# One layout for the loop's buffer ring, kept open to the end of the kernel

## The chip, the cores and the metric

The kernel runs on one core of a Trainium2 chip. The metric is the device time of one execution in microseconds. Before the change three runs took 781.46, 783.53 and 784.13 us; the median is 783.53.

## The reference, cut to what matters

Three stages follow one another, all in float32.

```python
# 1. attention, per batch and head: a local window of +-16 keys and 24 block summaries
k_sum, v_sum = k.reshape(B,H,nb,32,D).max(3), v.reshape(B,H,nb,32,D).mean(3)
a = softmax([q k^T / 8 inside the window, q k_sum^T / 8 + log 32])
attn = a @ [v, v_sum]                  # B, H, S, D = 4, 8, 768, 64
# 2. feed-forward: 3072 tokens, 512 -> 2048 -> 512
h = x @ w_in;  x = (h * cos(h)) @ w_out
# 3. soft mixture of 8 experts with 4 slots each
logits = x @ phi                       # 3072 x 32
d, c = softmax over tokens, softmax over slots
slot_out[e] = relu((d^T x)[e] @ w1[e]) @ w2[e]     # 512 -> 1024 -> 512
return c @ slot_out
```

## The kernel before

The feed-forward part is the backbone. It runs over 6 blocks of 512 tokens (NB) times 16 tiles of 128 hidden units (NF): 96 slots, and two more to drain. In slot s TensorE (PE) does mm1(s), 12 matmuls of 128x512 (L384, L385, L388), and mm2(s-2), 12 more (L425, L426, L429). Every operand is split in a high and a low float32r half, so a product takes three matmuls. Between them, DVE reduces the angle (L402, L403), ACT takes the sine (L404), DVE multiplies (L409, the tile `a`), ACT casts the high half (L412) and GpSimd (POOL) subtracts for the low half (L413). The weights of a later slot are split in the same way by `split_w`: ACT casts (L372), POOL, or in the first block DVE, subtracts (L373).

Around the backbone the attention of 24 groups (g) is spread, as background steps placed at given slots by `at` and `at2`: scores (sc), maximum (mx), exponentials, normalisation, transposes (tr, L336) that ACT copies (aT, L342), and the value product (av, L354), whose output is the x operand of mm1. Sums over 32 keys or values need loads of their own: kr (keys, reduced by DVE in L170 to ks) and vb (values, reduced by PE in L184 to vs, moved or added by DVE in L193 and L195). From the second batch on, all kr and vb loads go one after the other through one buffer, the tag `v2`: a load waits until the one before has been used. In the first block the 16 weight tiles (w0 to w15) also arrive packed as 64-bit numbers (raw, 1 MB each) and are converted in three steps, ACT (w and cv, L129, L130), DVE (a shift, L136) and POOL (an addition, L141).

After the loop comes the tail: expert weights are loaded in 64 transfers of 512 KB (`grab`, L532), each into a buffer that the loop has used up, and PE does the combine transposes (ct), the first expert product (hp, L809), the second (yp, L842) and the combine (op, L866), whose results leave in 12 transfers (L871).

The order of the work comes from two sources. Up to slot 17 (MAN0) a planner simulates a timeline and orders the instructions of all engines. From slot 17 on, PE and the queue of DMA issues (SP) take the written order, and the planner orders the other engines only. Inside an engine instructions run strictly in order: one that waits holds up everything behind it. A tile of a pool may be written again when all instructions that read it are done; two instructions that use different tiles don't wait for one another.

The parts that the change touches: the pool `ring` (2 buffers by default) with the tags `wih`, `wil`, `woh`, `wol` (hi and lo tiles of 2 KB a partition, 2 buffers each), `gh`, `gl` (3 buffers each) and `a`; the copies aT of the first four groups, which borrow tiles of that ring; the calls of `grab` at the end of the loop; and the pool `tail`, opened in the place of the closed ring, with 7 tiles r0 to r6 for expert weights and the tile cT0 for the first half of the combine operand.

Of the kernel before, what the change touches and what calls it, by code (L numbers as in the profile page):

```python
# [10 lines left out]
F32 = mybir.dt.float32  # L11
F32R = mybir.dt.float32r
# [18 lines left out]
TB = 512  # L31
# [17 lines left out]
NEXP = 12  # L49
WARM1 = 4  # L50
WARM2 = 4
NRING = 7
HB = (-4, 14)
HF = (-6, 10)
OA = 4
# [23 lines left out]
def body(ctx: ExitStack, tc: tile.TileContext, q0, qk, kT, vn, vx, w, phi, ex, cst, out):  # L79
# [7 lines left out]
    ps_acc = ctx.enter_context(tc.tile_pool(name="ps_acc", bufs=1, space=PSUM))  # L87
    ps_h = ctx.enter_context(tc.tile_pool(name="ps_h", bufs=2, space=PSUM))
    ps_m = ctx.enter_context(tc.tile_pool(name="ps_m", bufs=2, space=PSUM))
    ring_cm = tc.tile_pool(name="ring", bufs=2, side="right", reuse_waits="tile")  # L90
    ring = ring_cm.__enter__()
    att_cm = tc.tile_pool(name="att", bufs=2, reuse_waits="tile")
    att = att_cm.__enter__()

# [237 lines left out]
    def att_C(g, j):  # L332
        d = grp[g]
        ps = bank(f"tr{g}_{j}") if g < 4 else ps_m.tile([128, 512], F32, name=f"tr{g}_{j}", tag="m")
        for u in range(4):
            nc.tensor.transpose(ps[:KC, 128 * u:128 * u + 128], d["S"][:, 4 * j + u, :], ident)  # L336
        if g < 4:
            pool, tag, n = ring, ("gh", "gh", "gh", "gl", "gl", "gl", "a", "a")[2 * g + j], 2 if g == 3 else 3
        else:
            pool, tag, n = att, "aT", 2  # L340
        aT = pool.tile([KC, 512], F32, name=f"aT{g}_{j}", tag=tag, bufs=n)
        nc.scalar.copy(aT, ps[:KC, :])  # L342
        d["aT", j] = aT

# [22 lines left out]

    def split_w(f, part, eng=None):
        d, nm = ((wi, "wi"), (wo, "wo"))[part]
        hi = ring.tile([128, 512], F32R, name=f"{nm}h{f}", tag=nm + "h")  # L370
        lo = ring.tile([128, 512], F32R, name=f"{nm}l{f}", tag=nm + "l")
        nc.scalar.copy(hi, W[f][:, part, :])  # L372
        (eng or nc.gpsimd).tensor_tensor(out=lo, in0=W[f][:, part, :], in1=hi, op=ALU.subtract)  # L373
        d[f] = (hi, lo)
# [32 lines left out]
    def act2(s):  # L407
        h, a = hps.pop(s), gs[s]
        nc.vector.tensor_tensor(out=a, in0=h, in1=a, op=ALU.mult)  # L409
        gh = ring.tile([128, TB], F32R, name=f"gh{s}", tag="gh", bufs=3)  # L410
        gl = ring.tile([128, TB], F32R, name=f"gl{s}", tag="gl", bufs=3)
        nc.scalar.copy(gh, a)  # L412
        nc.gpsimd.tensor_tensor(out=gl, in0=a, in1=gh, op=ALU.subtract)  # L413
        gs[s] = (gh, gl)
# [265 lines left out]
    for s in range(NSLOT + LAG):  # L680
        if MAN is not None and s == MAN0:
            guard = tc.manual_schedule(engines=MAN)
            guard.__enter__()
        if s < NSLOT:
            mm1(s)
        if s + 1 < NSLOT:
            split_w((s + 1) % NF, 0, nc.vector if s + 1 < NF else None)
        if 0 <= s - LAG + 1 < NSLOT:
            split_w((s - LAG + 1) % NF, 1)
        if s < NSLOT:  # L690
            act1(s)
        fire(s, 0)
        if s < NSLOT:
            act2(s)
        if s >= LAG:
            mm2(s - LAG)
            if (s - LAG) % NF == NF - 1:
                last = [x2_out(t) for t in range(4)][3]
        fire(s, 1)
        fire(s, 2)  # L700
        if s - LAG >= NSLOT - NF:
            grab(wres, f"w{s - LAG - (NSLOT - NF)}")
    assert not bg, bg
    if guard:
        guard.__exit__(None, None, None)
    grab(xres, "xh", 2, bufs=2)
    grab(xres, "xl", 2, bufs=2)


    ring_cm.__exit__(None, None, None)  # L710
    tail = ctx.enter_context(tc.tile_pool(name="tail", bufs=1, side="right", reuse_waits="tile"))
    for i in range(NRING):
        grab(tail, f"r{i}")

    def cT_mm(j):

# [7 lines left out]
    def cT_split(j):  # L724

        ps = cps.pop(j)
        o = cT[j // 2][:, 512 * (j % 2):512 * (j % 2) + 512]
        nc.scalar.copy(o, ps)
        for r in (slice(32, 64), slice(96, 128)):
            nc.vector.tensor_tensor(out=o[r, :], in0=ps[r, :], in1=o[r, :], op=ALU.subtract)  # L730

    cps = {}
    cT = [tail.tile([128, 1024], F32R, name="cT0", tag="cT0")]


    with tc.issue_after(last.ins):
# [67 lines left out]
    for g in range(2):  # L804
        hp = [ps_acc.tile([128, 512], F32, name=f"hp{g}_{i}", tag=f"acc{2 * g + i}") for i in range(2)]
        for k in range(4):
            for i in range(2):
                for j in range(4):
                    nc.tensor.matmul(hp[i][32 * j:32 * j + 32, :], slT[:, k, :],  # L809
                                     eu[16 * g + 4 * k + j][0][:, 512 * i:512 * i + 512],  # L810
                                     start=k == 0, stop=k == 3)
            for j in range(4):
                release(16 * g + 4 * k + j, 2)
            if g == k == 0:
                cT.extend(place(f"cT{i}", F32R) for i in range(1, NB // 2))
                for j in range(2, NB):
                    cT_split(j)
        hr, t_ = place(f"hr{g}"), place(f"hT{g}").rearrange("p (k c) -> p k c", c=128)
# [14 lines left out]
    for h in range(2):  # L833
# [23 lines left out]
        for i in range(NB):  # L857
            pool, tag, kw = places[(NB * h + i) % 4]
            o = pool.tile([128, 4, 256], F32, name=f"o{h}_{i}", tag=tag, **kw)
            for t in range(2):  # L860
# [1 line left out]
                turn_o += 1  # L862
                ps = pool.tile([128, 512], F32, name=f"op{h}_{i}_{t}", tag=tag)
                for n in range(2):
                    k = 512 * (i % 2) + 256 * t + 128 * n
                    product = nc.tensor.matmul(ps[:, 256 * n:256 * n + 256], cT[i // 2][:, k:k + 128], so[:, c],  # L866
                                               start=True, stop=True)
                if i == 1:
                    before = slot_out, product
# [74 lines left out]
```

## Time and profile before

| | us |
|---|---|
| runs (3) | 781.46, 783.53, 784.13 |
| the profiled execution | 780.9 |
| its span, first to last instruction | 778.9 |
| PE busy | 740.2 |
| DVE busy | 473.6 |
| ACT busy | 433.4 |
| POOL busy | 428.6 |

The granted clock over the span is 0.987 of full speed. The profiled execution lies 2.6 us below the median of the runs. A time in the profile counts from the start of the span. Busy is the time in which an engine ran an instruction; matmuls are pipelined, so neighbouring ones overlap in the timeline, and their pitch is the distance of two starts. In the timeline, the bracket behind an instruction is the idle time of its engine just before it and what ended it.

### The profile page before, as it was taken

The numbers are of one execution on the slowest core, as the hardware profiler recorded it, in microseconds if no ns is written. First come the engines' busy times: TensorE is split into PE (matmuls) and PEld (weight loads), VectorE is DVE, ScalarE is ACT, GpSimd is POOL, SyncE is SP. The second block draws the span as 40 slices with busy tenths as digits, with TensorE's granted clock in tenths as the row PEclk, the third lists the DMA queues.
The fourth block names the chain that finished last, engine by engine and source line by source line (L and its number), as shares of the span: only waits on it lengthen the run. The fifth ranks groups of instructions, "written<-read, shape, count | busy, mean of one in ns | idle before, by whom it ended". The sixth has DMA issues, their size and how long they took to land.

```text
span 778.9 us, 13853 instructions
## 1 busy us (share of the span) xinstructions
PE 740.2 (95%) x5517; PEld 573.5 (74%) x5517; DVE 473.6 (61%) x686; ACT 433.4 (56%) x786; POOL 428.6 (55%) x302
## 2 busy tenths in 40 slices
PE   9977799998999999998999999999999999999994
PEld 7866678776877787776787777778768888786453
DVE  4578896767477576576575684774773444433523
ACT  4979868636465455574465555464554455443222
POOL 2555884365557657556566566665576665752000
PEclk9997999999999999999999999999999999999998
DMA  9988753121120331311211211301101922328978
GB/s 331 396 264 331 271 164 113 42 97 59 48 95 1 100 105 29 121 68 41 87 44 33 72 40 33 111 0 35 33 1 56 392 93 82 109 81 299 371 306 268
DMA packets 35585, 101.69 MB, mean 131 GB/s; under 512 B 3393, under 2 KB 13889, under 8 KB 33473
## 3 DMA queue, kind: packets, MB, share of 16 engines
q1 hardware_dynamic: 35520, 100.81, 36.8%
q8 instruction: 43, 0.70, 0.4%
q14 instruction: 22, 0.17, 0.1%
HBM read 92.54 MB, written 6.29 MB: 127 GB/s over the span
## 4 chain that ended last, share of the span: by engine, by line
PE 63%; DVE 13%; ACT 12%; DMA 6%; issue 4%; SPq 0%; ACTq 0%; DVEq 0%
PE acc L425 8%; PE h L384 8%; PE acc L426 8%; PE h L385 8%; PE acc L429 7%; PE h L388 7%; PE av L354 3%; DVE S L329 2%; DMA qk<-in_qk_dram 2%; PE yp L842 2%; DMA kr<-in_kT_dram 2%; PE sc L286 2%; PE hp L809 2%; ACT a L404 2%; DVE a L403 2%
## 5 line engine op out<-in xcount | busy, mean ns | idle before, releaser
L373 POOL TENSOR_TENSOR wol<-w,woh 128x512 fp32r<-128x512 f32 x96 | 143.9, 1500 | 115.0 <-ACT woh L372 115.0
L413 POOL TENSOR_TENSOR gl<-a,gh 128x512 fp32r<-128x512 f32 x96 | 129.0, 1343 | 83.8 <-ACT gh L412 78.3
L384 PE MATMUL h<-xh,wih 128*128 128x512 f32 x384 | 156.4, 407 | 6.7 <-DVE a L409 6.6
L425 PE MATMUL acc<-woh,gh 128*128 128x512 f32 x384 | 157.4, 410 | 3.5 <-DVE x L448 3.5
L385 PE MATMUL h<-xl,wih 128*128 128x512 f32 x384 | 152.2, 396 | 0.0
L426 PE MATMUL acc<-wol,gh 128*128 128x512 f32 x384 | 152.1, 397 | 0.0
L373 POOL TENSOR_TENSOR wil<-w,wih 128x512 fp32r<-128x512 f32 x81 | 113.9, 1406 | 42.8 <-PE h L388 24.2
L402 DVE TENSOR_SCALAR a<-h 128x512 f32<-128x512 f32 x96 | 65.9, 686 | 115.8 <-PE h L388 110.7
L404 ACT ACTIVATE a<-a,halfpi 128x512 f32<-128x512 f32 x96 | 69.4, 724 | 115.7 <-DVE a L403 115.4
L388 PE MATMUL h<-xh,wil 128*128 128x512 f32 x384 | 104.9, 395 | 0.0
L429 PE MATMUL acc<-woh,gl 128*128 128x512 f32 x384 | 104.6, 393 | 0.0
L409 DVE TENSOR_TENSOR a<-h,a 128x512 f32<-128x512 f32 x96 | 66.1, 689 | 57.0 <-ACT a L404 56.9
L425 PEld LDWEIGHTS acc<-woh,gh 128*128 128x128 f32 x384 | 72.4, 188 | 28.6 <-issue 11.8
L384 PEld LDWEIGHTS h<-xh,wih 128*128 128x128 f32 x384 | 72.7, 189 | 24.6 <-DVE a L409 8.4
L372 ACT CAST wih<-w 128x512 fp32r<-128x512 f32 x96 | 59.2, 617 | 47.2 <-PE h L385 46.4
L388 PEld LDWEIGHTS h<-xh,wil 128*128 128x128 f32 x384 | 72.5, 189 | 16.3 <-issue 0.2
L429 PEld LDWEIGHTS acc<-woh,gl 128*128 128x128 f32 x384 | 72.1, 189 | 16.4 <-issue 0.6
L385 PEld LDWEIGHTS h<-xl,wih 128*128 128x128 f32 x384 | 72.8, 190 | 15.2 <-issue 0.3
L426 PEld LDWEIGHTS acc<-wol,gh 128*128 128x128 f32 x384 | 72.6, 189 | 14.6 <-issue 0.6
L412 ACT CAST gh<-a 128x512 fp32r<-128x512 f32 x96 | 59.3, 619 | 32.8 <-DVE a L409 32.8
L372 ACT CAST woh<-w 128x512 fp32r<-128x512 f32 x96 | 59.1, 616 | 21.7 <-PE acc L429 20.8
L403 DVE SCALAR_TENSOR_TENSOR a<-a,h 128x512 f32<-128x512 f32 x96 | 65.5, 683 | 2.1
(137 smaller groups left out, 945.8 us busy)
## 6 DMA issues: line engine op xcount, KB each, us to landing
ex<-in_ex_dram SPq DMA_DIRECT2D x64, 512.0 KB
raw<-in_w_dram SPq DMA_DIRECT2D x16, 1024.0 KB
qk<-in_qk_dram SPq DMA_DIRECT2D x20, 736.0 KB
v<-in_vx_dram SPq DMA_DIRECT2D x24, 512.0 KB
kr<-in_kT_dram SPq DMA_DIRECT2D x16, 384.0 KB
vb<-in_vn_dram SPq DMA_DIRECT2D x12, 512.0 KB
out_dram<-o SPq DMA_DIRECT2D x12, 512.0 KB
v<-vs SPq DMA_DIRECT2D x40, 48.0 KB
```

The costliest lines, as they stand in the source:

```text
L372: nc.scalar.copy(hi, W[f][:, part, :])
L373: (eng or nc.gpsimd).tensor_tensor(out=lo, in0=W[f][:, part, :], in1=hi, op=ALU.subtract)
L384: nc.tensor.matmul(h, hi[:, c], xh[s // NF][:, t, :], start=t == 0, stop=False)
L385: nc.tensor.matmul(h, hi[:, c], xl[s // NF][:, t, :], start=False, stop=False)
L388: nc.tensor.matmul(h, lo[:, c], xh[s // NF][:, t, :], start=False, stop=t == 3)
L403: nc.vector.scalar_tensor_tensor(out=a, in0=a, scalar=MAGIC, in1=h, op0=ALU.subtract, op1=ALU.subtract)
L404: nc.scalar.activation(a, a, AF.Sin, bias=halfpi, scale=-TWO_PI)
L409: nc.vector.tensor_tensor(out=a, in0=h, in1=a, op=ALU.mult)
L413: nc.gpsimd.tensor_tensor(out=gl, in0=a, in1=gh, op=ALU.subtract)
L425: nc.tensor.matmul(acc[t], gh[:, c], hi, start=f == 0, stop=False)
L426: nc.tensor.matmul(acc[t], gh[:, c], lo, start=False, stop=False)
L429: nc.tensor.matmul(acc[t], gl[:, c], hi, start=False, stop=f == NF - 1)
```

## The change

The ring pool is not closed any more. Its hi and lo tiles become one tile of 4 KB a partition: `wi`, `wo` (2 buffers each) and `g` (3 buffers) in place of six tags. The two copies aT of each of the groups 0 to 2 share one tile `g`. The memory in use is the same. The pool `tail` is gone. In its place the last slots of the loop take the ring's tiles for expert weights: `wi` at slots 94 and 95, `xh` and `xl` at slot 95, `wo` at slots 96 and 97, `g` after the loop; the tiles w0 to w15 are taken one slot earlier in the code. The first two combine tiles cT live in the two `a` tiles.

```diff
--- before.py
+++ after.py
@@ -49,7 +49,6 @@
 NEXP = 12
 WARM1 = 4
 WARM2 = 4
-NRING = 7
 HB = (-4, 14)
 HF = (-6, 10)
 OA = 4
@@ -87,8 +86,7 @@
     ps_acc = ctx.enter_context(tc.tile_pool(name="ps_acc", bufs=1, space=PSUM))
     ps_h = ctx.enter_context(tc.tile_pool(name="ps_h", bufs=2, space=PSUM))
     ps_m = ctx.enter_context(tc.tile_pool(name="ps_m", bufs=2, space=PSUM))
-    ring_cm = tc.tile_pool(name="ring", bufs=2, side="right", reuse_waits="tile")
-    ring = ring_cm.__enter__()
+    ring = ctx.enter_context(tc.tile_pool(name="ring", bufs=2, side="right", reuse_waits="tile"))
     att_cm = tc.tile_pool(name="att", bufs=2, reuse_waits="tile")
     att = att_cm.__enter__()
 
@@ -335,10 +333,14 @@
         for u in range(4):
             nc.tensor.transpose(ps[:KC, 128 * u:128 * u + 128], d["S"][:, 4 * j + u, :], ident)
         if g < 4:
-            pool, tag, n = ring, ("gh", "gh", "gh", "gl", "gl", "gl", "a", "a")[2 * g + j], 2 if g == 3 else 3
+            if g == 3:
+                aT = ring.tile([KC, 512], F32, name=f"aT{g}_{j}", tag="a")
+            else:
+                if j == 0:
+                    d["aTs"] = ring.tile([KC, 2, 512], F32, name=f"aT{g}", tag="g", bufs=3)
+                aT = d["aTs"][:, j, :]
         else:
-            pool, tag, n = att, "aT", 2
-        aT = pool.tile([KC, 512], F32, name=f"aT{g}_{j}", tag=tag, bufs=n)
+            aT = att.tile([KC, 512], F32, name=f"aT{g}_{j}", tag="aT")
         nc.scalar.copy(aT, ps[:KC, :])
         d["aT", j] = aT
 
@@ -367,8 +369,8 @@
 
     def split_w(f, part, eng=None):
         d, nm = ((wi, "wi"), (wo, "wo"))[part]
-        hi = ring.tile([128, 512], F32R, name=f"{nm}h{f}", tag=nm + "h")
-        lo = ring.tile([128, 512], F32R, name=f"{nm}l{f}", tag=nm + "l")
+        hl = ring.tile([128, 2, 512], F32R, name=f"{nm}{f}", tag=nm)
+        hi, lo = hl[:, 0, :], hl[:, 1, :]
         nc.scalar.copy(hi, W[f][:, part, :])
         (eng or nc.gpsimd).tensor_tensor(out=lo, in0=W[f][:, part, :], in1=hi, op=ALU.subtract)
         d[f] = (hi, lo)
@@ -407,8 +409,8 @@
     def act2(s):
         h, a = hps.pop(s), gs[s]
         nc.vector.tensor_tensor(out=a, in0=h, in1=a, op=ALU.mult)
-        gh = ring.tile([128, TB], F32R, name=f"gh{s}", tag="gh", bufs=3)
-        gl = ring.tile([128, TB], F32R, name=f"gl{s}", tag="gl", bufs=3)
+        ghl = ring.tile([128, 2, TB], F32R, name=f"g{s}", tag="g", bufs=3)
+        gh, gl = ghl[:, 0, :], ghl[:, 1, :]
         nc.scalar.copy(gh, a)
         nc.gpsimd.tensor_tensor(out=gl, in0=a, in1=gh, op=ALU.subtract)
         gs[s] = (gh, gl)
@@ -698,19 +700,22 @@
                 last = [x2_out(t) for t in range(4)][3]
         fire(s, 1)
         fire(s, 2)
-        if s - LAG >= NSLOT - NF:
-            grab(wres, f"w{s - LAG - (NSLOT - NF)}")
+
+        f = s - LAG + 1 - (NSLOT - NF)
+        if 0 <= f < NF:
+            grab(wres, f"w{f}")
+        if NSLOT - 2 <= s < NSLOT:
+            grab(ring, "wi", bufs=2)
+        if s == NSLOT - 1:
+            grab(xres, "xh", 2, bufs=2)
+            grab(xres, "xl", 2, bufs=2)
+        if s >= NSLOT:
+            grab(ring, "wo", bufs=2)
     assert not bg, bg
     if guard:
         guard.__exit__(None, None, None)
-    grab(xres, "xh", 2, bufs=2)
-    grab(xres, "xl", 2, bufs=2)
-
-
-    ring_cm.__exit__(None, None, None)
-    tail = ctx.enter_context(tc.tile_pool(name="tail", bufs=1, side="right", reuse_waits="tile"))
-    for i in range(NRING):
-        grab(tail, f"r{i}")
+    for i in range(3):
+        grab(ring, "g", bufs=3)
 
     def cT_mm(j):
 
@@ -724,13 +729,15 @@
     def cT_split(j):
 
         ps = cps.pop(j)
-        o = cT[j // 2][:, 512 * (j % 2):512 * (j % 2) + 512]
+        if j < 2:
+            cT[j] = ring.tile([128, 512], F32R, name=f"cT{j}", tag="a")
+        o = cT[j]
         nc.scalar.copy(o, ps)
         for r in (slice(32, 64), slice(96, 128)):
             nc.vector.tensor_tensor(out=o[r, :], in0=ps[r, :], in1=o[r, :], op=ALU.subtract)
 
     cps = {}
-    cT = [tail.tile([128, 1024], F32R, name="cT0", tag="cT0")]
+    cT = {}
 
 
     with tc.issue_after(last.ins):
@@ -812,7 +819,9 @@
             for j in range(4):
                 release(16 * g + 4 * k + j, 2)
             if g == k == 0:
-                cT.extend(place(f"cT{i}", F32R) for i in range(1, NB // 2))
+                for i in range(2, NB, 2):
+                    t = place(f"cT{i}", F32R)
+                    cT[i], cT[i + 1] = t[:, 0:512], t[:, 512:1024]
                 for j in range(2, NB):
                     cT_split(j)
         hr, t_ = place(f"hr{g}"), place(f"hT{g}").rearrange("p (k c) -> p k c", c=128)
@@ -862,8 +871,8 @@
                 turn_o += 1
                 ps = pool.tile([128, 512], F32, name=f"op{h}_{i}_{t}", tag=tag)
                 for n in range(2):
-                    k = 512 * (i % 2) + 256 * t + 128 * n
-                    product = nc.tensor.matmul(ps[:, 256 * n:256 * n + 256], cT[i // 2][:, k:k + 128], so[:, c],
+                    k = 256 * t + 128 * n
+                    product = nc.tensor.matmul(ps[:, 256 * n:256 * n + 256], cT[i][:, k:k + 128], so[:, c],
                                                start=True, stop=True)
                 if i == 1:
                     before = slot_out, product
```

In the changed kernel the lines between about L104 and L333 are numbered 2 lower and those of the loop 2 higher (L384 is L386, L532 is L534); the tile names lose their h and l, so a cast and a subtraction both write wi5, wo2 or g2.

The change moves instructions where the planner orders them. First ACT, in slot 2. aT4_0 is the copy of group 4's first transpose, w9 and cv9 belong to the conversion of weight tile 9, a2 is the sine of slot 2. Before:

```order
L404 ACTIVATE a2_853<-a2_853,halfpi_90 128x512
L372 CAST wih5_1013<-w5_817 128x512
L342 COPY aT4_0_866<-tr4_0_861 120x512
L129 ACTIVATE w9_1103<-raw9_958 128x1024
L130 ACTIVATE cv9_1104<-raw9_958 128x1024
L412 CAST gh2_888<-a2_853 128x512
L372 CAST woh2_934<-w2_583 128x512
```

After:

```order
L406 ACTIVATE a2_842<-a2_842,halfpi_90 128x512
L127 ACTIVATE w9_1083<-raw9_944 128x1024
L128 ACTIVATE cv9_1084<-raw9_944 128x1024
L344 COPY aT4_0_855<-tr4_0_850 120x512
L414 CAST g2_877<-a2_842 128x512
L374 CAST wo2_921<-w2_580 128x512
L374 CAST wi5_998<-w5_809 128x512
```

The copy now stands behind the conversion of w9, and the cast of weight 5's first half (wih5, now wi5) has moved from in front of both to behind the cast of wo2.

Next DVE, in slots 3 and 4. vs1 is the value sum of the second batch, w11 and w12 are shifts of the conversion, a4 the angle of slot 4. Before:

```order
L136 TENSOR_SCALAR w11_1251<-w11_1251 128x1024
L195 TENSOR_TENSOR vs1_877<-vs1_877,vs1_1_942 128x128
L402 TENSOR_SCALAR a4_1021<-h4_1000 128x512
L403 SCALAR_TENSOR_TENSOR a4_1021<-a4_1021,h4_1000 128x512
L373 TENSOR_TENSOR wil6_1092<-w6_879,wih6_1091 128x512
L136 TENSOR_SCALAR w12_1309<-w12_1309 128x1024
L409 TENSOR_TENSOR a4_1021<-h4_1000,a4_1021 128x512
L363 TENSOR_TENSOR xl1_995<-av4_977,xh1_994 128x2x256
```

After:

```order
L411 TENSOR_TENSOR a3_924<-h3_905,a3_924 128x512
L134 TENSOR_SCALAR w11_1225<-w11_1225 128x1024
L404 TENSOR_SCALAR a4_1004<-h4_985 128x512
L405 SCALAR_TENSOR_TENSOR a4_1004<-a4_1004,h4_985 128x512
L375 TENSOR_TENSOR wi6_1073<-w6_868,wi6_1073 128x512
L411 TENSOR_TENSOR a4_1004<-h4_985,a4_1004 128x512
L134 TENSOR_SCALAR w12_1280<-w12_1280 128x1024
L193 TENSOR_TENSOR vs1_866<-vs1_866,vs1_1_928 128x128
L134 TENSOR_SCALAR w13_1355<-w13_1355 128x1024
```

The addition to vs1 stood right behind the shift of w11; now four operations of slot 4, among them the subtraction for wi6, and the shift of w12 stand in front of it. On PE the matmuls vs1_1 that it waits for moved with it, from inside mm1(4) to the start of mm1(5).

DVE again, in slots 7 and 8. mx6 is the row maximum of group 6, ks11 the last key reduction of the third batch. Before:

```order
L409 TENSOR_TENSOR a7_1224<-h7_1203,a7_1224 128x512
L290 SCALAR_TENSOR_TENSOR S6_1230<-sc6_1_1232,mask2_571 128x480
L298 TENSOR_REDUCE mx6_1276<-S6_1230 128x8
L402 TENSOR_SCALAR a8_1301<-h8_1280 128x512
L170 TENSOR_REDUCE ks11_1732<-kr11_1613 128x24
```

After:

```order
L411 TENSOR_TENSOR a7_1198<-h7_1179,a7_1198 128x512
L288 SCALAR_TENSOR_TENSOR S6_1204<-sc6_1_1206,mask2_568 128x480
L168 TENSOR_REDUCE ks11_1685<-kr11_1571 128x24
L296 TENSOR_REDUCE mx6_1249<-S6_1204 128x8
L404 TENSOR_SCALAR a8_1272<-h8_1253 128x512
```

ks11 has moved in front of mx6 and of slot 8's first step.

## Rows read from the trace of the kernel before

**Rows 1.** The page, part 1: engine, busy us, share of the span, instructions

```profile
PE 740.2 (95%) x5517; PEld 573.5 (74%) x5517; DVE 473.6 (61%) x686; ACT 433.4 (56%) x786; POOL 428.6 (55%) x302
```

**Rows 2.** Stretches: length, busy us (PE PEld DVE ACT POOL), clock, DMA share

```profile
80.00:100.00 20.00, 15.70 (x118) 11.94 (x117) 17.63 (x17) 16.51 (x24) 19.11 (x10) 0.91 0.76 271
...
180.00:200.00 20.00, 17.04 (x122) 13.20 (x120) 15.24 (x22) 12.53 (x21) 12.64 (x10) 1.00 0.08 27
200.00:700.00 500.00, 490.91 (x3201) 388.20 (x3200) 303.74 (x436) 270.05 (x442) 310.73 (x225) 1.00 0.22 74
720.00:750.00 30.00, 29.53 (x383) 14.47 (x386) 13.62 (x31) 5.78 (x13) 0.00 (x0) 1.00 1.00 386
```

**Rows 3.** Waits of PE and ACT, 200 to 705: us in total, times, longest

```profile
PE h L384 <- DVE a L409: 3.4, 3, 1.1
...
ACT wih L372 <- PE h L385: 43.1, 45, 1.8
```

**Rows 4.** Timeline of PE: start, us, line, operation, idle time before and releaser

```profile
78.09 0.65 PE L336 MATMUL tr<-ident,S 128*120 128x128 f32 x4
...
85.04 1.15 PE L354 MATMUL av<-aT,v 120*64 120x64 f32 x32 [1.36 <-ACT aT L342]
89.13 0.77 PE L336 MATMUL tr<-ident,S 128*120 128x128 f32 x4 [2.94 <-DVE vs L195]
...
90.55 0.63 PE L425 MATMUL acc<-woh,gh 128*128 128x512 f32 x1
90.98 0.63 PE L426 MATMUL acc<-wol,gh 128*128 128x512 f32 x1
...
98.48 0.65 PE L184 MATMUL vs<-vb,avg 128*32 128x128 f32 x16
...
100.26 0.40 PE L384 MATMUL h<-xh,wih 128*128 128x512 f32 x1
100.49 0.40 PE L385 MATMUL h<-xl,wih 128*128 128x512 f32 x1
...
139.90 0.50 PE L384 MATMUL h<-xh,wih 128*128 128x512 f32 x1
```

**Rows 5.** The line that issues the expert loads: ns min/median/max, first and last

```profile
L532 SPq DMA_DIRECT2D ex<-in_ex_dram x64: 327/328/1144, 587.5 to 744.0; - x64
```

**Rows 6.** Timeline of ACT, slot 2

```profile
77.46 0.58 ACT L342 COPY aT<-tr 120x512 f32<-120x512 f32 x1
77.94 1.15 ACT L129 ACTIVATE w<-raw 128x1024 f32<-128x1024 f32 x1
78.99 1.14 ACT L130 ACTIVATE cv<-raw 128x1024 int32<-128x1024 uint32 x1
```

**Rows 7.** Timeline of DVE, slots 2 to 10

```profile
79.11 0.69 DVE L136 TENSOR_SCALAR w<-w 128x1024 int32<-128x1024 int32 x1 [1.15 <-ACT w L129]
...
88.80 0.27 DVE L195 TENSOR_TENSOR vs<-vs,vs 128x128 f32<-128x128 f32 x1
...
90.32 1.52 DVE L373 TENSOR_TENSOR wil<-w,wih 128x512 fp32r<-128x512 f32 x1
91.76 2.87 DVE L136 TENSOR_SCALAR w<-w 128x1024 int32<-128x1024 int32 x1
...
116.84 1.15 DVE L298 TENSOR_REDUCE mx<-S 128x8 f32<-128x960 f32 x1
...
120.28 0.95 DVE L170 TENSOR_REDUCE ks<-kr 128x24 f32<-128x768 f32 x1 [1.05 <-DMA kr<-in_kT_dram]
...
124.80 0.69 DVE L409 TENSOR_TENSOR a<-h,a 128x512 f32<-128x512 f32 x1 [1.96 <-ACT a L404]
...
139.15 0.69 DVE L409 TENSOR_TENSOR a<-h,a 128x512 f32<-128x512 f32 x1 [0.69 <-ACT a L404]
```

**Rows 8.** Timeline of POOL, the addition beside DVE's shift

```profile
91.24 2.83 POOL L141 TENSOR_TENSOR w<-w,cv 128x1024 int32<-128x1024 int32 x1
```

**Rows 9.** The chain that ended last, 50 to 200: start, us, what

```profile
99.18 5.24 DMA kr<-in_kT_dram
```

## The prediction

> **What bounds the kernel now.** I read the page's first part, then the busy times by stretch, then the lists of waits, and last the timelines of the one place where TensorE (PE) idles and the change touches. PE is busy 740.2 us of a span of 778.9 [rows 1], so at most 38.7 us can be had without removing a matmul, and the change removes none. In the long middle of the loop PE is busy 490.91 of 500 us at a granted clock of 1.00 [rows 2]: a slot (12 + 12 matmuls) simply takes its 24 matmul pitches, and PE waits there for DVE's gelu product in only 3 places, 3.4 us together [rows 3]. In the tail stretch 720 to 750, where the DMA engines are full (share 1.00), PE is still busy 29.53 of 30 us [rows 2]. Idle PE time of a size that matters lies early: in 80 to 100 us it is busy only 15.70 of 20, and the clock there is 0.91 [rows 2]. The timeline names the stalls: 1.36 us before the value product of group 4 (at 85.04) and 2.94 us before a transpose of group 5 (at 89.13), after which matmuls stand 0.43 us apart (90.55, 90.98) in place of 0.23 (100.26, 100.49) [rows 4].
>
> **The change, part by part.**
>
> *Tail: the expert loads.* The same 64 loads go out [rows 5]; the issue order shows other buffers and one load that leaves a slot earlier. Expert weights are read by PE in the tail, and PE idles for 0.47 us in the stretch where the loads still run [rows 2]. What comes earlier there finds nobody waiting: 0. From both sides: the gain there cannot pass that 0.47; the loss, if an early load takes bandwidth from another, I put at the same size, since the rows show none. The two transposed combine tiles now live in the gelu product's own buffers; these were last read before the loop's last 12 matmuls, so they are free long before: 0.
>
> *Steady loop: one tile for hi and lo.* A weight tile is now free when both halves have been read. The hi cast on ACT, which waited for the last L385 (45 waits, 43.1 us [rows 3]), now waits for the last L388, four matmuls of 0.23 us or 0.92 us later. Behind it on ACT stands the sine of the same slot, which needs that same L388 and then two DVE operations, so nothing ready is held up. PE needs the cast after a further 36 matmuls (mm2, mm1, mm2), 36 x 0.23 = 8.3 us, and the list of its waits names neither the cast nor the subtraction [rows 3]. Cost 0. If that cover failed, PE would wait up to 0.92 us in a slot, and the first 17 slots are where ACT is dense enough for it.
>
> *The first slots: a new order.* Slots before 17 are put in order by a planner, and the changed tiles give it another plan; this is where I expect the time to move. Three instructions matter.
> (1) ACT's copy of group 4's first transpose stood before the conversion of weight tile 9 (77.46; conversion at 77.94 and 78.99 [rows 6]) and now stands behind it. With the wi cast also gone from before it, w9 starts at 76.95, the copy at 79.05 and it ends at 79.63. PE comes to the second transpose, which reuses that bank, at 78.09 [rows 4], or 78.55 with the two matmuls now ahead of it: about +1.1 us.
> (2) The matmuls of vs1_1 stood inside mm1(4) and now stand behind mm2(2) and before group 4's value product. That product then comes some 2 us later (87.3), and its copy, which I place at 84.6 on ACT, is done by then: -1.36.
> (3) DVE's addition of vs1_1, which releases the bank of the group-5 transpose, ran at 88.80 [rows 7]; now a4's steps, the lo half of weight 6 and the shift of weight 12 stand before it. ACT, walked on with its durations, has cast weight 6 at about 88.8; then come the lo half, 1.5, the product, 0.6, and the shift, 0.7 to 2.9 [rows 7], of which I take 1.2: the addition at about 92.1. PE, with mm2(2) and mm1(5) moved ahead (87.3, the value product 1.1, ten matmuls 2.3), reaches the transpose at about 90.7: it waits some 1.5 in place of 2.94.
> Without the long gap I take the clock to stay up: ten matmuls at 0.43 in place of 0.23 and a slower transpose were 2.1 us. So mm1(6) comes at 100.26 + 1.1 - 1.36 - 2.94 + 1.5 - 2.1 = 96.5, some 4 us earlier.
>
> In the dense stretch, DVE's shift of a weight tile takes 0.69 us at 79.11 and 2.87 at 91.76, beside GpSimd's addition of 2.83 at 91.24 [rows 7, 8]; (3) depends on which of these fall together. The Trainium skill (SBUF — State Buffer, "Who interferes with whom") says that DVE's second port pair is shared with GpSimd and whoever comes first holds it for its whole instruction; the trace agrees with 2.87 against 0.69. By that rule, with every DVE step of (3) blocked as it was from 88.80 on, the addition would come at 94.9 (the shift ended at 94.6; 0.6 more for the product, 0.3 less for the addition itself), PE would wait 4.2, and nothing would be kept: 783.5.
>
> *What is left of it.* The earlier PE meets the one serial chain that did not move. The last vs matmuls (98.48 [rows 4]) release the single buffer into which the next key load (5.24 us at 99.18 [rows 9]) goes; then load, reduction and the next load follow one another, to ks11 at 120.28 [rows 7]. In the new order these vs matmuls stand right behind mm1(6), 96.5 + 2.8 = 99.3, 0.8 later than before. DVE meets the reductions in its order, so it cannot run ahead of them. What can be saved there is DVE's idle time: 1.05 before ks11 and 1.96 before the product of slot 8 [rows 7]. ks11 now stands before the group's row maximum (116.84), which then comes about 0.8 us later, if kr11's load starts early enough. Of the 3.0 us of idle time I take off 0.8 for the later key chain and 0.3 for what ks11 ahead of the maximum still costs behind it on ACT: 1.9. The product of slot 10 then ends at about 138.0. It ended at 139.84 and mm1(12) started at 139.90 [rows 4, 7], with no slack: this is where PE's time is set. So 1.9 of the 4 us are kept. All that follows has the same order on PE and is carried along.
>
> Sum: 780.9 (profiled execution) - 1.9 = 779.0. The median of the runs, 783.53, stands 2.6 above that execution; 779.0 + 2.6 = 781.6.
> Bounds of the whole: below, the two stalls and the slow clock gone with only the new copy wait added, 1.36 + 2.94 + 2.1 - 1.1 = 5.3 of gain; above, the price of the third rival, 4.3 of loss.
>
> **Rivals.**
> *The whole early gain survives.* DVE, no longer tied up, reduces kr8 to kr11 in time, and slot 10's product is as early as mm1(6) was: 4 to 5.3 us, 778 to 779.5. For it: PE's stretch 100 to 139 has no stall of its own in the rows. Against it: slot 10's product follows ACT's sine (0.69 us of idle before it at 139.15 [rows 7]), behind exponentials that wait for the same DVE.
> *Nothing is kept.* The new wait (3) is as long as the old one, or the key chain sets mm1(12) as before: 783.5.
> *Slower: ks11 ahead of the maximum.* If kr11 lands when it did, ks11 runs at 120.28 and ends at 121.2; the maximum behind it then starts there and not at 116.84, 4.3 us later, and so do the exponentials of group 6, slot 8's sine behind them on ACT and slot 10's product. DVE's idle 1.96 takes up part of it: +2.3 to +4.3, 786 to 788. It decides from the moment kr11 lands later than 117.5. For it: the vs matmuls that start the chain come later, and the chain has single buffers. Against it: on DVE the reductions before it stand no later than they did, and less waits in front of them.
> *The clock.* If one of the waits that I leave (1.1 and 1.5) lowers the clock as the 2.94 did, 2.1 us more go in that stretch. Against it: in 180 to 200 PE is idle 2.96 us in all and the clock stays at 1.00 [rows 2]. By then mm1(6) is at 98.6 and the key chain starts 2 us later: about 783.5 again. The Trainium skill (TensorE: Matmul & The Clock Gate, "HAM oscillation — how this bites in real kernels") has idle gaps between bursts of matmuls as what throttles the array; the rows at 89.13 agree, those of 180 to 200 show gaps that did not.
>
> **Chances.** Forecast 0.40 (own range 779.5 to 783.5); whole gain 0.20; nothing kept, the clock's case with it, 0.19; slower 0.21. A measurement of this kernel tells 0.3% from no change, 2.35 us: faster is below 781.2, slower above 785.9. Faster: 0.20 and half of the forecast's 0.40, 0.40. Same: the other half and the 0.19, 0.39. Slower: 0.21. Eight in ten lie between 777.0 (the whole gain less a little run spread) and 787.0 (most of the slower case).
>
> **What would show it.** Right: in 80 to 100 us PE shows no stall before the value product, one of 1 to 2 us before the group-5 transpose, one of about 1 before the second transpose of group 4, and a clock near 1.00; mm1(12) at about 138; from there every slot as before, shifted by the same amount; PE's tail stretch as full as before with loads that went out earlier. Wrong: mm1(12) before 136 (the chain did not bind) or after 141 (ks11 did); new waits of PE for ACT's or GpSimd's halves in 200 to 700, which would mean that the merged tiles cost; or a tail whose length differs by more than 0.5 us.

## The result, and the profile after

The changed kernel takes 785.79 us (median of 12 runs, 785.05 to 787.53) against 780.48 (12 runs, 779.17 to 784.13): ratio 1.0064, 95% interval 1.005 to 1.0077. It is slower by 5 us, where 2 us faster was forecast; the time lies inside the range, on the side of the third rival, which had 0.21.

The profiled executions are 780.9 and 785.87 us, their spans 778.9 and 783.7. Where the 4.8 us between the spans arise is read from the starts of the first matmul of mm1(s) in the timelines of PE:

| start of | before | after | difference |
|---|---|---|---|
| mm1(4) | 79.53 | 79.89 | +0.36 |
| mm1(6) | 100.26 | 95.51 | -4.75 |
| mm1(9) | 121.02 | 117.75 | -3.27 |
| mm1(10) | 127.72 | 129.91 | +2.19 |
| mm1(11) | 133.25 | 137.48 | +4.23 |
| mm1(12) | 139.90 | 143.81 | +3.91 |
| mm1(16) | 168.78 | 173.35 | +4.58 |
| mm1(95) | 699.01 | 703.84 | +4.83 |
| end of the span | 778.9 | 783.7 | +4.8 |

The loss is all but complete at slot 16. The 79 slots behind it take 530.23 us before and 530.49 after, and from mm1(95) to the end it is 79.9 us in both. The first part of the page and the stretches (the clock stands in the third place from the end) say the same:

```profile
PE 742.0 (95%) x5517; PEld 574.6 (73%) x5517; DVE 469.0 (60%) x686; ACT 432.1 (55%) x786; POOL 426.7 (54%) x302
```

```profile
80.00:100.00 20.00, 18.19 (x136) 13.86 (x135) 16.45 (x17) 15.78 (x22) 19.32 (x11) 1.00 0.89 333
...
120.00:140.00 20.00, 14.69 (x82) 11.37 (x82) 13.77 (x22) 15.17 (x47) 5.63 (x4) 0.83 0.28 107
180.00:200.00 20.00, 17.04 (x92) 13.15 (x91) 15.06 (x21) 13.42 (x21) 10.61 (x9) 1.00 0.16 56
200.00:700.00 500.00, 490.59 (x3230) 388.19 (x3229) 304.83 (x437) 270.54 (x443) 311.19 (x225) 1.00 0.22 73
725.00:755.00 30.00, 29.71 (x386) 14.60 (x389) 13.44 (x30) 5.61 (x12) 0.00 (x0) 1.00 0.90 343
```

The stretch 80 to 100 has gained: 18.19 us busy against 15.70, at a clock of 1.00 against 0.91 [rows 1, 2]. The stretch 120 to 140 lost it and more: 14.69 busy at 0.83; it was 19.92 at 1.00 in the kernel before:

```profile
120.00:140.00 20.00, 19.92 (x119) 15.88 (x117) 13.64 (x22) 16.18 (x45) 6.80 (x5) 1.00 0.21 65
```

The long middle and the tail (725 to 755, the same work as 720 to 750 before) are as they were.

The timeline of PE in those places:

```profile
78.92 0.65 PE L334 MATMUL tr<-ident,S 128*120 128x128 f32 x4 [0.63 <-ACT aT L344]
...
84.34 1.18 PE L428 MATMUL acc<-wo,g 128*128 128x512 f32 x4 [0.60 <-POOL wo L375]
...
87.40 1.15 PE L356 MATMUL av<-aT,v 120*64 120x64 f32 x32
...
92.25 0.65 PE L334 MATMUL tr<-ident,S 128*120 128x128 f32 x4 [1.21 <-DVE vs L193]
...
95.51 0.40 PE L386 MATMUL h<-xh,wi 128*128 128x512 f32 x1
...
98.37 0.64 PE L182 MATMUL vs<-vb,avg 128*32 128x128 f32 x16
...
129.91 0.79 PE L386 MATMUL h<-xh,wi 128*128 128x512 f32 x1 [5.31 <-DVE a L411]
130.50 0.63 PE L387 MATMUL h<-xl,wi 128*128 128x512 f32 x1
130.93 0.63 PE L386 MATMUL h<-xh,wi 128*128 128x512 f32 x1
...
137.48 0.40 PE L386 MATMUL h<-xh,wi 128*128 128x512 f32 x1
```

Up to the row at 98.37 this is what the forecast said [rows 4]: the wait before the second transpose, none before the value product at 87.40, a short one before the group-5 transpose, full clock. Only the wait of 0.60 us at 84.34, for POOL's half of wo, was not in it. Then one row decides: 5.31 us of idle time before mm1(10), and matmuls at half clock behind it (0.43 from 130.50 to 130.93), so that mm1(10) with mm2(8) takes 7.57 us and not 5.53. DVE shows what PE waits for:

```profile
91.92 0.27 DVE L193 TENSOR_TENSOR vs<-vs,vs 128x128 f32<-128x128 f32 x1
...
116.19 0.65 DVE L288 SCALAR_TENSOR_TENSOR S<-sc,mask 128x480 f32<-128x480 f32 x1
121.06 0.95 DVE L168 TENSOR_REDUCE ks<-kr 128x24 f32<-128x768 f32 x1 [4.22 <-DMA kr<-in_kT_dram]
121.93 1.14 DVE L296 TENSOR_REDUCE mx<-S 128x8 f32<-128x960 f32 x1
...
129.16 0.69 DVE L411 TENSOR_TENSOR a<-h,a 128x512 f32<-128x512 f32 x1 [1.08 <-ACT a L406]
```

The first row is the addition to vs1, forecast for 92.1. In the third, ks11 waits 4.22 us for kr11's load, and the maximum of group 6 (L296), whose scores were ready after the row at 116.19, runs at 121.93; before it ran at 116.84 [rows 7]. The exponentials of group 6, the sine of slot 8 behind them on ACT, and slot 8's product follow: 129.16 against 124.80.

Why the load came so late stands in the queue of DMA issues. Before (start, time that the entry held the queue, the line's tile):

```profile
105.43 0.34 SPq L165 DMA_DIRECT2D kr<-in_kT_dram  x1
107.80 0.33 SPq L219 DMA_DIRECT2D v<-in_vx_dram  x1
109.52 0.33 SPq L165 DMA_DIRECT2D kr<-in_kT_dram  x1
112.93 1.66 SPq L229 DMA_DIRECT2D v<-vs  x2
...
115.67 0.33 SPq L165 DMA_DIRECT2D kr<-in_kT_dram  x1
```

After:

```profile
107.56 4.41 SPq L163 DMA_DIRECT2D kr<-in_kT_dram  x2
112.06 0.38 SPq L217 DMA_DIRECT2D v<-in_vx_dram  x1
115.98 1.65 SPq L227 DMA_DIRECT2D v<-vs  x2
117.73 0.46 SPq L163 DMA_DIRECT2D kr<-in_kT_dram  x1
```

Before, v7's load (107.80) goes out in front of kr10's. After, kr9 and kr10 stand one behind the other (the row at 107.56 holds both, the second one waiting for ks9), v7's load goes out 4.3 us later at 112.06, its copies from vs, which wait for that load to land, at 115.98, and kr11's load behind them at 117.73, though ks10 had released the buffer at 115.67.

How much of mx6's lateness is the load's? From its issue to the reduction kr11 took 3.3 us (117.73 to 121.06), and 4.6 us before (115.67 to 120.28), so ks11 ran only 0.8 us later than before. Of the 5.1 us by which mx6 is late, 4.3 come from its new place behind ks11 and 0.8 from the later landing.

In the loop, the wait of the wi cast that I priced at nothing doubled, and nothing came of it (waits of PE and of ACT, 200 to 705) [rows 3]:

```profile
PE h L386 <- DVE a L411: 3.4, 3, 1.2
...
ACT wi L374 <- PE h L390: 87.8, 48, 2.8
```

### The profile page after: what moved, and what is told of

Read it like the earlier page. It is cut to its first block, busy times and chain, and to the rows that moved or that the text cites. A ratio compares the mean times of both kernels' runs of the same rounds, so it can differ in the third digit from the quotient of the medians.

```text
span 783.7 us, 13781 instructions
## 1 busy us (share of the span) xinstructions
PE 742.0 (95%) x5517; PEld 574.6 (73%) x5517; DVE 469.0 (60%) x686; ACT 432.1 (55%) x786; POOL 426.7 (54%) x302
## 4 chain that ended last, share of the span: by engine, by line
PE 57%; ACT 15%; DVE 14%; DMA 8%; issue 5%; SPq 1%; ACTq 0%; DVEq 0%
PE h L386 8%; PE acc L427 7%; PE h L387 7%; PE h L390 7%; PE acc L428 7%; PE acc L431 7%; PE av L356 3%; DVE S L327 2%; ACT a L406 2%; PE yp L851 2%; DVE a L405 2%; DMA raw<-in_w_dram 2%; ACT S L305 2%; PE hp L816 2%; PE sc L284 2%
## 5 line engine op out<-in xcount | busy, mean ns | idle before, releaser
L375 POOL TENSOR_TENSOR wo<-w,wo 128x512 fp32r<-128x512 f32 x96 | 142.8, 1488 | 104.1 <-ACT wo L374 104.1
L415 POOL TENSOR_TENSOR g<-a,g 128x512 fp32r<-128x512 f32 x96 | 129.4, 1348 | 84.0 <-ACT g L414 83.9
L386 PE MATMUL h<-xh,wi 128*128 128x512 f32 x384 | 157.9, 411 | 12.2 <-DVE a L411 12.1
L427 PE MATMUL acc<-wo,g 128*128 128x512 f32 x384 | 156.7, 409 | 3.7 <-DVE x L450 3.7
L387 PE MATMUL h<-xl,wi 128*128 128x512 f32 x384 | 153.1, 399 | 0.0
L428 PE MATMUL acc<-wo,g 128*128 128x512 f32 x384 | 150.8, 394 | 0.6 <-POOL wo L375 0.6
L375 POOL TENSOR_TENSOR wi<-w,wi 128x512 fp32r<-128x512 f32 x81 | 112.3, 1386 | 62.0 <-ACT wi L374 61.8
L374 ACT CAST wi<-w 128x512 fp32r<-128x512 f32 x96 | 59.3, 618 | 98.3 <-PE h L390 97.3
L390 PE MATMUL h<-xh,wi 128*128 128x512 f32 x384 | 105.8, 397 | 0.0
L431 PE MATMUL acc<-wo,g 128*128 128x512 f32 x384 | 104.2, 392 | 0.0
L386 PEld LDWEIGHTS h<-xh,wi 128*128 128x128 f32 x384 | 73.4, 191 | 30.9 <-DVE a L411 14.6
L427 PEld LDWEIGHTS acc<-wo,g 128*128 128x128 f32 x384 | 72.1, 188 | 28.6 <-issue 10.7
L390 PEld LDWEIGHTS h<-xh,wi 128*128 128x128 f32 x384 | 73.0, 190 | 16.4 <-issue 0.2
L387 PEld LDWEIGHTS h<-xl,wi 128*128 128x128 f32 x384 | 73.5, 191 | 15.2 <-issue 0.3
L431 PEld LDWEIGHTS acc<-wo,g 128*128 128x128 f32 x384 | 71.9, 188 | 16.4 <-issue 0.7
L428 PEld LDWEIGHTS acc<-wo,g 128*128 128x128 f32 x384 | 72.2, 188 | 15.2 <-POOL wo L375 1.0
```

The source lines that it names most:

```text
L386: nc.tensor.matmul(h, hi[:, c], xh[s // NF][:, t, :], start=t == 0, stop=False)
L387: nc.tensor.matmul(h, hi[:, c], xl[s // NF][:, t, :], start=False, stop=False)
L390: nc.tensor.matmul(h, lo[:, c], xh[s // NF][:, t, :], start=False, stop=t == 3)
L427: nc.tensor.matmul(acc[t], gh[:, c], hi, start=f == 0, stop=False)
L428: nc.tensor.matmul(acc[t], gh[:, c], lo, start=False, stop=False)
L431: nc.tensor.matmul(acc[t], gl[:, c], hi, start=False, stop=f == NF - 1)
```

## The experiments

Theory: two changes of order in the first block, made by the planner, cost the time: kr11's load late on the DMA queue, and ks11 ahead of mx6 on DVE, which hands the lateness on. Rivals: the later release of the merged tiles costs slot by slot (A); the tail's earlier loads cost (B). Where an edit says "issue_after", it fixes the order of issue on one engine and asks for no other wait. All ratios are against the kernel before, run on the same chip beside them.

**ks11 behind mx6.** DVE's order at one place; PE, POOL and SP keep the changed kernel's order exactly, ACT and DVE swap a few neighbours behind it.

```diff
-        nc.vector.reduce_max(out=ks, in_=ksums[n]...
+        with tc.issue_after(maxes[6].ins) if n == 11 else nullcontext(): nc.vector.reduce_max(out=ks, in_=ksums[n]...
```

> The changed kernel with one order fixed on DVE: the reduction ks11 is issued behind the row maximum mx6, nothing else is asked for. Theory (ks11 ahead of mx6 holds DVE in a wait for kr11's load): the 4.2 us wait in front of mx6 goes, mx6 runs near 117, slot 8's product near 124.5, PE's stall of 5.3 us before mm1(10) shrinks to 1 or less, the clock stays at 1.00 in 120 to 140, mm1(12) starts near 138 in place of 143.8, and the time falls from 785.8 to about 779 to 780. Rival A (the later release of the merged weight tiles costs the time slot by slot) and rival B (the tail's loads cost it): no change, 785 to 786.

780.55 us (778.59 to 785.01), ratio 1.0001 (0.9984 to 1.0018): 5.2 us below the changed kernel, so the whole loss is gone, though the time is a little above the 779 to 780 expected. DVE, and the stretch 120 to 140:

```profile
116.71 1.15 DVE L296 TENSOR_REDUCE mx<-S 128x8 f32<-128x960 f32 x1
...
120.23 0.95 DVE L168 TENSOR_REDUCE ks<-kr 128x24 f32<-128x768 f32 x1 [1.77 <-DMA kr<-in_kT_dram]
...
125.04 0.69 DVE L411 TENSOR_TENSOR a<-h,a 128x512 f32<-128x512 f32 x1 [0.55 <-ACT a L406]
```

```profile
120.00:140.00 20.00, 20.00 (x120) 16.16 (x119) 15.56 (x24) 18.34 (x50) 8.42 (x6) 1.00 0.25 90
```

ks11 still waits for its load, but behind mx6, which runs at 116.71. PE is busy all of that stretch at full clock, and mm1(12) starts at 138.00, the place that the forecast gave. A and B fall: nothing of the merged tiles or of the tail was touched.

**v7's load ahead of kr10's**, on the queue only; DVE has one swap of neighbours, ACT, PE and POOL none.

```diff
-        nc.sync.dma_start(out=t, in_=kT[n])
+        with tc.issue_after(vload[7].ins) if n == 10 else nullcontext(): nc.sync.dma_start(out=t, in_=kT[n])
```

> The changed kernel with one order fixed on the queue of DMA issues: v7's load goes out before kr10's again, as in the kernel before. Theory: kr11's load, which stood behind the v7 copies in that queue until 117.7, goes out near 115.7, so ks11 and mx6 behind it come 1 to 2 us earlier, PE's stall before mm1(10) is 3.3 to 4.5 in place of 5.3, and the time is 784 to 785. If the wait is set by the load's own duration and not by the queue: the stall stays at 5.3 and the time at 785.8. Rivals A and B: 785.8.

782.3 us, ratio 1.0023 (1.0012 to 1.0034), 3.5 below the changed kernel, more than expected. The queue and DVE:

```profile
107.37 0.46 SPq L217 DMA_DIRECT2D v<-in_vx_dram  x1
110.94 0.33 SPq L163 DMA_DIRECT2D kr<-in_kT_dram  x1
...
115.36 0.33 SPq L163 DMA_DIRECT2D kr<-in_kT_dram  x1
```

```profile
118.52 0.95 DVE L168 TENSOR_REDUCE ks<-kr 128x24 f32<-128x768 f32 x1 [2.63 <-DMA kr<-in_kT_dram]
119.39 1.14 DVE L296 TENSOR_REDUCE mx<-S 128x8 f32<-128x960 f32 x1
```

kr11 goes out 2.4 us earlier, at 115.36, and ks11, though still in front of mx6, runs at 118.52, earlier than in the kernel before (120.28), because the load itself took 3.2 us here and 4.6 there. The stall before mm1(10) is 3.3 us:

```profile
127.38 0.50 PE L386 MATMUL h<-xh,wi 128*128 128x512 f32 x1 [3.34 <-DVE a L411]
```

**kr11 in a buffer of its own.** ks11 stays in front of mx6.

```diff
-            t = att.tile([128, S], F32, name=f"kr{n}", tag="v2", bufs=1)
+            t = (m2 if n in (11,) else att).tile([128, S], F32, name=f"kr{n}", tag="x2T" if n in (11,) else "v2", bufs=1)
```

> The changed kernel with kr11 loaded into a buffer that is free by then (the one that holds x2T later) and not into the shared one: ks11 still stands in front of mx6 on DVE (now even in front of slot 7's product), but its load no longer waits for ks10. Theory (the load's lateness behind ks10 and the queue makes the wait, the place in front of mx6 passes it on): no wait of DVE for kr11, mx6 near 117, no stall of PE before mm1(10) above 1 us, clock 1.00 in 120 to 140, time as with ks11 behind mx6: 779.5 to 781.5. If the place alone cost (0.95 us of DVE in front of mx6 and the product): 781.5 to 782.5. Merged tiles or tail as causes: 785 to 786.

781.29 us, ratio 1.0021 (1.0001 to 1.0041). ks10 and ks11 run back to back without a wait (one row, x2), and mx6 at 117.19:

```profile
114.18 1.81 DVE L168 TENSOR_REDUCE ks<-kr 128x24 f32<-128x768 f32 x2
...
117.19 1.15 DVE L296 TENSOR_REDUCE mx<-S 128x8 f32<-128x960 f32 x1
```

So the place in front of mx6 costs little when the load is there; it is the load's lateness that it hands on. One thing did not come as expected: PE still waits 2.11 us before mm1(10), where at most 1 was expected, and the clock stays at 1.00. The other buffer also lets the next vb load go out earlier (117.19 against 122.04), so this run changes more than the one wait.

```profile
126.39 0.51 PE L386 MATMUL h<-xh,wi 128*128 128x512 f32 x1 [2.11 <-DVE a L411]
```

**The kernel before, with mx6 behind ks11.**

```diff
-        nc.vector.reduce_max(out=ks, in_=ksums[n]...
+        r_ = nc.vector.reduce_max(out=ks, in_=ksums[n]...
+        n == 11 and tc.add_manual_dep(maxes[6].ins, r_.ins.name, ..., reason="issue_after")
```

> The kernel before, with all its tiles and its tail, and only the row maximum mx6 issued behind ks11 on DVE (the planner then also moves some operations of slots 8 to 12). Theory: ks11 at about 120.3, mx6 at 121.2 in place of 116.84, PE stalls some 3 to 5 us before mm1(10), the clock falls to half for a slot, mm1(12) comes 4 to 5 us later, and the time is 784 to 786 against 780.5. Rivals A and B: no merged tile and no early load here, so 780.5.

782.56 us, ratio 1.0028 (1.0017 to 1.0039): slower, by 2 and not by 4 to 6. DVE and PE:

```profile
119.76 0.94 DVE L170 TENSOR_REDUCE ks<-kr 128x24 f32<-128x768 f32 x1
120.62 1.14 DVE L298 TENSOR_REDUCE mx<-S 128x8 f32<-128x960 f32 x1
...
127.34 0.69 DVE L409 TENSOR_TENSOR a<-h,a 128x512 f32<-128x512 f32 x1 [2.18 <-ACT a L404]
```

```profile
128.09 0.50 PE L384 MATMUL h<-xh,wih 128*128 128x512 f32 x1 [0.53 <-DVE a L409]
...
132.59 0.53 PE L425 MATMUL acc<-woh,gh 128*128 128x512 f32 x1 [1.47 <-ACT gh L412]
```

mx6 is nearly as late as expected (120.62, expected 121.2), and slot 8's product 2.5 us later than before. But PE meets it with 0.53 us of idle time and 1.47 at a later place, because in this kernel PE itself comes to mm1(10) only at 127.5; in the changed kernel it was there 3 us earlier, at 124.6. The expectation took the loss from the changed kernel's stall, more than half of which is the lead that PE gave back. The planner also gave ACT two more table loads here, so this run does not show the single order alone.

**The tail undone**: the weight tiles taken a slot later, the ring's tiles only after the loop.

```diff
-        f = s - LAG + 1 - (NSLOT - NF)
+        f = s - LAG - (NSLOT - NF)
-        if NSLOT - 2 <= s < NSLOT:
-            grab(ring, "wi", bufs=2)
...
+    for t_ in ("wi", "wi", "wo", "wo", "g", "g", "g"): grab(ring, t_, bufs=3 if t_ == "g" else 2)
```

> The changed kernel with the early expert loads undone: the weight tiles are taken a slot later, as before, and the ring's tiles only after the loop. Theory: PE waits for no expert load in either kernel, so 785.3 to 786.3, with the stall before mm1(10) as in the changed kernel. Rival B (the early loads collide with something): back by up to 5 us, 781 to 783. If the early loads gain something that the first block's loss hides: up to 1 us slower, 786.5 to 787.

784.55 us, ratio 1.0055 (1.0041 to 1.0069), beside 1.0064 (1.005 to 1.0077) with the early loads: no difference that can be told (785.3 to 786.3 was expected). From mm1(95) (701.95) to the end of the span (781.8) it is 79.9 us again. The stall before mm1(10) is 5.1 us.

**Which tile made the new plan.** The kernel before with wi merged alone, all else as before:

```diff
+        if part == 0:
+            hl = ring.tile([128, 2, 512], F32R, name=f"{nm}{f}", tag=nm)
+            hi, lo = hl[:, 0, :], hl[:, 1, :]
```

> The kernel before with one part of the change alone: the hi and lo halves of the first weights (wi) in one tile; gelu and second weights, tail and expert loads as before. In the planner's order this part alone brings kr10's load in front of v7's, ks11 in front of mx6 and the addition to vs1 behind the shift of weight 12. Theory (the later release of this tile changes the plan, and the plan costs): the whole loss is here, 784.5 to 786.5, with PE's stall of about 5 us before mm1(10) and the tail as long as before (79.9 us from mm1(95) to the end). Rival (the tail or the other merged tiles take part): 780.5 to 783.

785.32 us, ratio 1.0066 (1.0054 to 1.0079): the whole loss. Up to the end of the loop the order on all five engines is that of the changed kernel. PE's waits up to 200 us (total, times, longest):

```profile
PE h L388 <- DVE a L413: 8.9, 4, 5.5
```

**wo and g merged alone**, with the shared copies of the first groups:

```diff
-        gh = ring.tile([128, TB], F32R, name=f"gh{s}", tag="gh", bufs=3)
-        gl = ring.tile([128, TB], F32R, name=f"gl{s}", tag="gl", bufs=3)
+        ghl = ring.tile([128, 2, TB], F32R, name=f"g{s}", tag="g", bufs=3)
+        gh, gl = ghl[:, 0, :], ghl[:, 1, :]
...
+        if part == 1:
+            hl = ring.tile([128, 2, 512], F32R, name=f"{nm}{f}", tag=nm)
```

> The kernel before with the other two parts of the ring's new layout alone: hi and lo of the second weights in one tile, hi and lo of the gelu product in one tile, shared by the copies of the first groups; wi in two tiles, tail and expert loads as before. The first block's order on DVE, ACT, POOL and SP is that of the kernel before. Theory: no cost, 779.5 to 781.5, mm1(12) at 139 to 140.5. Rival (merged tiles hold something up in every slot): some 0.05 us a slot, 784 to 786.

780.18 us, ratio 1.0 (0.9987 to 1.0013): nothing; the order on every engine is that of the kernel before, and mm1(12) starts at 139.32. So of the change's parts only the later release of the wi tile acts, and it acts through the plan. Where the plan turns off can be read from the order alone, and it is earlier than the moves of slot 2 on ACT: the cast of weight 3's first half already stands behind a group's exponentials (60.11 in the changed kernel), where it stood in front of them (57.43). Why the planner then chose the rest is not shown.

**Versions that try to keep the early lead.** All three have ks11 behind mx6. The first also issues the shift of weight 12 behind the addition to vs1; the second, in addition, the conversion of weight tile 9 behind group 4's first copy; the third, in addition, has kr11's own buffer. The planner moves more with them: in the first two v7's load stands in front of kr10's again.

```diff
+        with tc.issue_after(vadd[1, 1].ins) if f == 12 else nullcontext(): nc.vector.tensor_single_scalar(out=wi_, ...
```

> The changed kernel with ks11 behind mx6 and, in slot 4, the shift of weight 12 issued behind the addition to vs1 on DVE. Theory: PE's wait before the group-5 transpose (1.2 in the changed kernel, 2.4 with ks11 moved) falls below 1, the clock keeps 1.00 in 80 to 100, mm1(6) comes 1 to 3 us earlier than with ks11 moved alone (97.6); but slot 8's product was only 0.4 us ahead of PE there, so mm1(12) gains 0.3 to 2: 778.5 to 780.5 against 780.55. If DVE and ACT set mm1(12) fully: the same 780.5. If the planner's other moves cost: 781 to 782.

781.06 us, ratio 1.0009 (0.9985 to 1.0033): no gain. The wait before the group-5 transpose stayed at 1.45 us (PE was there earlier, too), and mm1(12) started at 137.91 after a wait of 1.81 for slot 10's product: that product sets the time.

```diff
+        with tc.issue_after(aTc[4, 0].ins) if f == 9 else nullcontext(): nc.scalar.activation(W[f], raw[f]...
```

> As the kernel with the addition to vs1 moved, and on ACT in slot 2 the conversion of weight tile 9 issued behind the copy of group 4's first transpose. Theory: PE's wait before the second transpose (0.6 to 1.6) goes, mm1(4) comes about 1 us earlier; of that, what slot 8's product allows is kept: 0 to 1 us below the kernel without it, 778 to 780. If only the place where time is set moves: equal.

779.15 us (777.35 to 781.19), ratio 0.9975 (0.9961 to 0.9988): faster than both kernels, by 0.25% than the one before. PE:

```profile
88.87 0.65 PE L334 MATMUL tr<-ident,S 128*120 128x128 f32 x4 [0.84 <-DVE vs L193]
...
136.40 0.50 PE L386 MATMUL h<-xh,wi 128*128 128x512 f32 x1 [1.46 <-DVE a L411]
```

The wait before the group-5 transpose is 0.84, mm1(6) starts at 93.04, and mm1(12) at 136.40, again behind slot 10's product.

```diff
-            t = att.tile([128, S], F32, name=f"kr{n}", tag="v2", bufs=1)
+            t = (m2 if n in (11,) else att).tile([128, S], F32, name=f"kr{n}", tag="x2T" if n in (11,) else "v2", bufs=1)
```

> As the kernel with the copy moved, and kr11 in a buffer of its own. Theory: ks11's wait for its load (1.8 us of DVE, behind slot 8's first step) goes, slot 8's product comes up to 1 us earlier, and more of PE's lead is kept: 777 to 779.5. If exponentials on ACT set that product and not DVE: equal to the kernel without it.

780.02 us, ratio 0.9992 (0.9979 to 1.0005): no gain over the kernel before is left to see, though the interval overlaps that of the second version. ks11 has no wait, but the order on the other engines is another again: PE now waits 1.80 us at 102.23 for an addition to vs on DVE, which was not there, and mm1(12) starts at 138.95. The expectation looked at ks11's wait only.

## Why the prediction was wrong

Right were the frame and most steps. The tail is worth 0: 79.9 us in all twelve kernels profiled here. The merged tiles cost 0 in the loop: the cast's wait grew from 43.1 to 87.8 us, PE's waits for the product stayed at 3.4. The first block decides. In it (1) was 0.63 us where 1.1 was said, (2) came as said, (3) was 1.21 where 1.5 was said, the clock stayed at 1.00, and mm1(6) came at 95.51 where 96.5 was said.

That mm1(6) came so near is in part luck, because errors of the sum cancel. It lacks the wait of 0.60 us for POOL. It prices the slow clock at 2.1 us, where the ten matmuls took 3.96 us (89.55 to 93.51) and 2.3 at full clock, so 1.7. And it doesn't take off the vs matmuls and the transpose that the new order put behind mm1(6), 1.0 us (98.48 to 99.46 before), though it names the move of the vs matmuls. At mm1(9), where both kernels have done the same work, the lead is 3.27 and not 4.75.

The step that failed is the one under "What is left of it": ks11 in front of the maximum, "which then comes about 0.8 us later, if kr11's load starts early enough". It did not: mx6 came 5.1 us later. The 0.8 is what the forecast had for the lateness of the key chain; what mx6 pays is the whole way from its old start, 116.84, to the end of ks11. With kr11 landing just as before, that is 4.3 us by the rows of the kernel before. Two things were left out besides. The chain was followed through the shared buffer (load, reduction, next load) and not through the queue of DMA issues, where the new order had put kr10's load in front of v7's; the copies that wait for v7 then stood in front of kr11. And the condition was passed by with the remark that on DVE the reductions stood no later and less waited in front of them; in fact ks8 and ks9 ran at 106.59 and 110.65, 2.1 us later than before. The third rival said from which moment it decides: kr11 landing after 117.5. It landed at about 121. That rival is what happened, at its place and by its mechanism, and the sign named for it came, mm1(12) after 141: 143.81. Its range, +2.3 to +4.3, was too low because it left out the half clock behind the stall: mm1(10) with mm2(8) took 2.04 us longer. Counted from mm1(9): PE had a lead of 3.27, lost it and 2.19 more at mm1(10) by the stall of 5.31, and 2.04 by the clock.

That the time lies inside the stated range is luck too. The forecast added 2.6 us, by which the median of three runs, 783.53, stood above the profiled execution. The median of twelve is 780.48, a little below that execution. Counted from there the forecast is 778.6 and the range about 774 to 784, and 785.79 lies outside it.

With that one order put right, mm1(12) started at 138.00, the forecast's figure, and the time was still 780.55, equal to the kernel before: in the median of several runs the lead of 1.9 does not show. The agreement at 138.00 is chance: in that execution slot 10's product was done at 137.38 and PE came after it, having lost time earlier. There the group-5 transpose waits 2.38 us, not 1.21, and the clock falls behind it. ACT and DVE show why:

```profile
89.57 1.14 ACT L127 ACTIVATE w<-raw 128x1024 f32<-128x1024 f32 x1 [0.91 <-DMA raw<-in_w_dram]
```

```profile
90.75 1.78 DVE L134 TENSOR_SCALAR w<-w 128x1024 int32<-128x1024 int32 x1 [0.56 <-ACT w L127]
```

The conversion of weight 12 waits 0.91 us for its load, which it did not in the changed kernel; the shift behind it starts late and takes 1.78 us, not 1.19, and the addition to vs1 follows at 92.46. The order on ACT, DVE and the queue up to there is that of the changed kernel, so this lateness belongs to the execution. Whether it is also what the median pays stays open: this execution, 779.09, is faster than the median.

## What to carry to other kernels

A change of buffers can act through the order alone: one release four matmuls later gave another plan for 17 slots, and two swaps in it cost 5 us while the change's own waits cost nothing. So read the new order on every in-order queue, the one of DMA issues included, and for each instruction that moved forward ask when its own input lands; one that may wait belongs behind those that are ready. When PE's early stall goes away, look for the next place where its time is set, here slot 10's product: the lead is only worth what that place leaves.

## What the runs showed of the hardware

The granted clock fell to its lower level behind idle gaps of PE of 5.31 us (changed kernel) and 3.3 us (v7's load moved), as behind the 2.94 before, and also behind 2.38, in the version with ks11 moved (PE, pitch 0.42 from 93.78 to 94.20, 0.23 at full clock):

```profile
92.79 0.65 PE L334 MATMUL tr<-ident,S 128*120 128x128 f32 x4 [2.38 <-DVE vs L193]
...
93.78 0.63 PE L427 MATMUL acc<-wo,g 128*128 128x512 f32 x1
94.20 0.63 PE L428 MATMUL acc<-wo,g 128*128 128x512 f32 x1
```

It kept its upper level behind 1.21 us in the changed kernel, behind 1.45 and 1.81 in the first of the last three versions, and behind 2.11 with kr11 in its own buffer. What such a stretch costs can be read from mm1(10) with mm2(8): 5.53 us at full clock before, 7.57 in the changed kernel, 7.02 with the tail undone and 8.35 with wi merged alone, so 1.5 to 2.8 us.
